# The first 768-token block's second product by seven block products, and its combined weights made four stages earlier

## The chip, the cores and the metric

The kernel runs on one core of a Trainium2 chip. The core has five instruction queues that run side by side and wait for each other through semaphores: TensorE (PE, matrix products into PSUM banks), VectorE (DVE), ScalarE (ACT), GpSimd (POOL) and SyncE (SP). Here SP issues all the transfers between the chip's memory (HBM) and the on-chip buffer (SBUF). Each engine takes its instructions strictly in the order in which they were written for it. The metric is the device time of one execution in microseconds (us); the time of a kernel is the median over its runs.

## The reference, cut to what matters

Pooled attention (keys and values are averaged over groups of 8) followed by a two-layer product with a gate between. Everything is float32.

```python
k_p = k.reshape(B, H, Sp, 8, D).mean(axis=3)          # B=8, H=8, Sp=72, D=64
v_p = v.reshape(B, H, Sp, 8, D).mean(axis=3)
attn = softmax(q @ k_p.T / sqrt(D))                    # 576 queries per head
x = (attn @ v_p) -> 4608 tokens x 512
h = x @ w_in                                           # 512 x 2048
g = h * clip(h + 3, 0, 6) / 6
out = g @ w_out                                        # 2048 x 512
```

## The kernel before, in words

The 4608 tokens are worked in blocks: `BLOCKS = [512, 256, 384, 384] + [384] * 8`. The first four blocks, numbered 0 to 3, are "plain"; the last eight are taken in pairs of 384 as four 768-token blocks. PE does its products on float32 data that have been rounded to a shorter form, so each operand is split into a rounded part (`hi`, written by ACT) and the remainder (`lo`, `q` minus `hi`, written by DVE), and each product is three: hi·hi, hi·lo, lo·hi. Attention for later tokens is fed in small steps between the products of earlier blocks.

**Plain blocks.** `run` goes over 16 steps, one for each 128 of the 2048 hidden columns. A step has the first product (`Step.h`, L841, 12 products into one of two PSUM banks), its gate (`relu` on ACT L849, `gate` on DVE L853), its split (`hi` on ACT L857, `lo` on DVE L861), and two steps later the second product (`Step.out`, L872, three products for each 128 tokens). Before a block's first step its tokens must be split too: `split_x`, ACT L624 and DVE L625, which writes `xhi` and `xlo`. `hooks[j][u]` holds work that is called after step `u` of block `j`.

**768-token blocks.** Their first product, `h`, is done by the seven-product form of a 2x2 block product (L1134): three of the seven right-hand operands are raw blocks of the weights, four are sums and differences of blocks ("combined weights"). In the last three of these blocks the second product, `out`, is done by seven products too (`out_seven`, L1261, 28 pieces of 3 x 6 products of 128x256 elements, 504 in all). In the first of them it is done plainly (`out_plain`, L1188, 16 pieces of 6 x 3 products of 128x512, 288 in all). All weights that the 768-token blocks need lie in HBM, in `wd` (for `h`), `w2d` (raw, for `out`) and `w2t` (combined, for `out`), and are read back through two rings of buffers (`chunk`, L992).

**Who makes the combined weights.** Those for `h` are made by `sums_of`, in 16 halves: eight in block 2 and eight in block 3, at every second step. A half is, in one go, two additions (L939), four dependent mixes (L944), the rounded copy on ACT (L945), the remainder (L946), and four stores of 128 KB (L948). Its buffer `wq` exists once, so the next half's first addition waits until the stores have read it. Those for `out` are made by `combine` (L1017, L1020, L1022, L1023, stores L1026) while the first 768-token block does its plain `out`: they read the pieces that are loaded for `out` anyway. `plain_of` stores the raw weights of blocks 2 and 3's hooks to HBM (L951); nothing that it reads changes, so these stores can be issued early.

**What sets the order.** Up to step 3 of block 1 the order on each engine is a written list. After it, the order comes from the scheduler of the language, which places each engine's instructions by its own estimate of when they are ready. `after_mark` adds the rule that an instruction stands behind the last marked one (the split of the latest step) on its engine. The SBUF that block 1's pool `early_x0` occupied is handed to the pool `early_x1` of blocks 2 and 3 when block 1's last step is reached; a tile that is put there waits for the last users of what lay there.

## Time and profile before

| | us |
|---|---|
| median of 3 runs (lowest to highest) | 893.26 (893.08 to 894.79) |
| the profiled execution | 893.88 |
| its span, first to last instruction | 892.1 |
| PE busy / DVE busy / ACT busy in the span | 869.2 / 665.9 / 553.6 |
| block 0 | 0 to 126 |
| block 1 | 126 to 184 |
| block 2 | 184 to 269 |
| block 3 | 269 to 346 |
| first 768-token block: `h`, then plain `out` | 346 to 423, 423 to 494 |
| second: `h`, `out` by seven | 494 to 566, 566 to 633 |
| third: `h`, `out` by seven | 633 to 704, 704 to 769 |
| fourth: `h`, `out` by seven | 769 to 828, 828 to 888 |

The stages' edges are the first products of the lines named above. The profile is of one execution; its rows give an engine, a line of the kernel, an operation, the tiles written and read, and busy time. A row of a timeline begins with its start and its length in us. A row of a table by stages gives a stretch of the span, its length, the busy time of PE, of its weight loads (PEld), of DVE, ACT and POOL, each with the count of instructions, then the granted share of the PE clock, the mean busy share of the 16 transfer engines, and GB/s.

### The profile page before, as it was taken

Reading aid. Unit: us, or ns where it says so; the run is one execution under the profiler, and the core shown is the slowest. Engines: PE = TensorE matmul, PEld = TensorE weight load, DVE = VectorE, ACT = ScalarE, POOL = GpSimd, SP = SyncE. Lnnn points to the kernel's source line nnn. Section 1 sums busy time; section 2 is a strip of 40 time slices with the busy share of each in tenths; the row PEclk is TensorE's granted clock in tenths of the full one; section 3 lists DMA queues with packets and bytes.
Section 4 is the critical chain, followed back from the end, with each engine's and each line's share of the span. In section 5 each row is a group of like instructions: output and inputs, shape, how many; then the busy total and the mean of one; then the engine's idle time right before and its main releaser. Section 6 shows DMA issues by size and latency. Waiting matters only on the chain.

```text
span 892.1 us, 15646 instructions
## 1 busy us (share of the span) xinstructions
PE 869.2 (97%) x5360; PEld 812.3 (91%) x5360; DVE 665.9 (75%) x1340; ACT 553.6 (62%) x1515; POOL 83.6 (9%) x168
## 2 busy tenths in 40 slices
PE   7899999999999999999999999999999999999998
PEld 6788888988989998998888999999999999999998
DVE  6999864567877785869788688897597877466664
ACT  5998766655656655778344688665577746355442
POOL 4100002110211100102000101100100200000000
PEclk9999999999999999999999999999999999999999
DMA  9970205995425234996587968877976777877873
GB/s 294 392 293 1 72 24 192 360 327 167 130 67 160 71 129 135 368 315 225 180 271 239 383 218 295 265 239 236 331 250 213 226 233 240 275 253 238 266 264 132
DMA packets 124654, 200.00 MB, mean 224 GB/s; under 512 B 13216, under 2 KB 81056, under 8 KB 124576
## 3 DMA queue, kind: packets, MB, share of 16 engines
q1 hardware_dynamic: 124432, 199.00, 67.8%
q8 instruction: 43, 0.70, 0.3%
q14 instruction: 35, 0.29, 0.1%
q10 hardware_dynamic: 144, 0.00, 0.0%
HBM read 158.08 MB, written 40.89 MB: 223 GB/s over the span
## 4 chain that ended last, share of the span: by engine, by line
PE 80%; DVE 8%; DMA 5%; ACT 4%; issue 2%; SPq 1%; POOL 0%; DVEq 0%; ACTq 0%; POOLq 0%
PE psx L1134 22%; PE psx L1261 19%; PE pso L872 12%; PE psh L841 12%; PE psx L1188 7%; PE psa L646 3%; PE psa L463 3%; ACT e L472 2%; PE psa L572 1%; DMA raw<-w_in_l 1%; DMA raw<-w_out_l 1%; DMA wd<-wq 1%; DVE vst L383 1%; DMA wsFalse<-wd 1%; DVE wq L939 1%
## 5 line engine op out<-in xcount | busy, mean ns | idle before, releaser
L1134 PE MATMUL psx<-x,wsFalse 128*128 128x384 f32 x768 | 151.8, 341 | 1.7 <-DVE g L1098 0.8
L841 PE MATMUL psh<-xhi,w 128*128 128x384 f32 (+2 forms) x520 | 145.9, 340 | 0.5 <-DVE g L853 0.4
L1134 PEld LDWEIGHTS psx<-x,wsFalse 128*128 128x128 f32 x768 | 133.6, 188 | 3.2 <-ACT c L1107 1.3
L1113 ACT CAST part<-g 128x768 fp32r<-128x768 f32 x100 | 83.3, 836 | 85.0 <-PE psx L1261 65.8
L1115 DVE TENSOR_TENSOR part<-g,part 128x768 fp32r<-128x768 f32 x100 | 95.2, 955 | 46.5 <-ACT part L1113 46.1
L872 PE MATMUL pso<-w,ghi 128*128 128x512 f32 x384 | 120.7, 398 | 0.4 <-ACT o L877 0.4
L1134 PE MATMUL psx<-x,wsTrue 128*128 128x384 f32 x576 | 115.8, 342 | 2.4 <-DMA wsTrue<-wd 2.3
L1261 PE MATMUL psx<-wsFalse,part 128*128 128x256 f32 x864 | 108.3, 282 | 1.5 <-DVE part L1115 1.1
L1261 PEld LDWEIGHTS psx<-wsFalse,part 128*128 128x128 f32 x864 | 105.2, 189 | 2.3 <-DVE part L1115 1.3
L1134 PEld LDWEIGHTS psx<-x,wsTrue 128*128 128x128 f32 x576 | 99.6, 188 | 3.1 <-DVE g L1092 3.1
L841 PEld LDWEIGHTS psh<-xhi,w 128*128 128x128 f32 x520 | 93.2, 188 | 8.2 <-DVE g L853 1.1
L472 ACT ACTIVATE e<-psa,mx 128x72 f32<-128x72 f32 x256 | 78.6, 324 | 23.7 <-DVE mx L467 22.4
L841 PE MATMUL psh<-xlo,w 128*128 128x384 f32 (+2 forms) x260 | 87.1, 336 | 0.0
L501 POOL TENSOR_TENSOR a<-e,sm 128x256 f32<-128x256 f32 x60 | 41.0, 683 | 478.3 <-DVE sm L490 377.9
L1261 PE MATMUL psx<-wsTrue,part 128*128 128x256 f32 x648 | 81.3, 283 | 0.0
L1261 PEld LDWEIGHTS psx<-wsTrue,part 128*128 128x128 f32 x648 | 79.3, 191 | 0.2 <-DVE part L1115 0.2
L872 PEld LDWEIGHTS pso<-w,ghi 128*128 128x128 f32 x384 | 69.1, 188 | 11.2 <-ACT o L877 0.7
L1090 ACT ACTIVATE r<-g,small 128x384 f32<-128x384 f32 x96 | 58.8, 621 | 28.4 <-DVE g L1098 28.0
L872 PE MATMUL pso<-w,glo 128*128 128x512 f32 x192 | 74.4, 399 | 0.0
L1098 DVE TENSOR_TENSOR g<-psx,c 128x384 f32<-128x384 f32 x96 | 52.3, 553 | 28.7 <-PE psx L1134 20.6
L1107 ACT COPY c<-psx 128x384 f32<-128x384 f32 x96 | 45.0, 485 | 28.5 <-PE psx L1134 28.1
L1092 DVE SCALAR_TENSOR_TENSOR g<-r,g 128x384 f32<-128x384 f32 x96 | 54.5, 576 | 9.7 <-ACT r L1090 9.2
(139 smaller groups left out, 1473.2 us busy)
## 6 DMA issues: line engine op xcount, KB each, us to landing
wsFalse<-wd SPq DMA_DIRECT2D x64, 512.0 KB, 4.6
wsTrue<-wd SPq DMA_DIRECT2D x48, 512.0 KB, 4.9
wsFalse<-w2d SPq DMA_DIRECT2D x31, 512.0 KB, 5.0
wsFalse<-w2t SPq DMA_DIRECT2D x27, 512.0 KB, 5.0
wsTrue<-w2d SPq DMA_DIRECT2D x21, 512.0 KB, 5.0
wsTrue<-w2t SPq DMA_DIRECT2D x21, 512.0 KB, 4.9
raw<-w_in_l SPq DMA_DIRECT2D x16, 512.0 KB, 8.6
raw<-w_out_l SPq DMA_DIRECT2D x16, 512.0 KB, 9.2
```

What stands on the lines that cost most here:

```text
L472: nc.scalar.activation(self.e[:, h], self.ps[:, h], AF.Exp, bias=self.mx[:, h : h + 1], accum_out=self.sm[:, h : h + 1])
L841: nc.tensor.matmul(self.ps, l[f][:, c, :], r[:, c, :], start=c == 0 and i == 0, stop=c == NCC - 1 and i == 2)
L872: nc.tensor.matmul(pos, l, r, start=f == 0 and i == 0, stop=f == NF - 1 and i == 2)
L1090: nc.scalar.activation(r, src, AF.Relu, bias=half_low, scale=GSCALE / (6.0 * WSCALE))
L1092: nc.vector.scalar_tensor_tensor(out=g_of[i][:, k], in0=r, scalar=GSCALE, in1=src, op0=ALU.min, op1=ALU.mult)
L1098: nc.vector.tensor_tensor(out=g_of[i][:, k], in0=ps, in1=kept, op=ALU.add)
L1107: nc.scalar.copy(c, ps)
L1113: nc.scalar.copy(t[:, 0], src)
L1115: nc.vector.tensor_tensor(out=t[:, 1], in0=src, in1=t[:, 0].bitcast(F32), op=ALU.subtract)
L1134: nc.tensor.matmul(ps, w[:, l, c * P : (c + 1) * P], t[:, r, c], start=o in (1, 2, 5) and c == 0 and k == 0, stop=c == 1 and k == 2, skip_ ...
L1188: nc.tensor.matmul(to, l, w[:, qs, r], start=f == 0 and k == 0, stop=end and k == 2)
L1261: nc.tensor.matmul(to, t[:, l, k, i * P : (i + 1) * P], w[:, k, r], start=begin and k == 0 and y == 0 and i % 2 == 0, stop=m == NM - 1 and ...
```

## The change

All four 768-token blocks do `out` by seven products; `out_plain` and `combine` are gone. The combined weights for `out` are now made from the resident weights in block 3 (`sums_of_out`, eight pieces of 4 x 128x256, in buffers of steps that block 3 has finished with). The combined weights for `h` move earlier: the first half of them (four whole pieces of 128x512 additions, through the space of `xlo` of block 0) into block 1, the second half (eight halves as before) into block 2. Each is cut in two parts: additions, mixes and the rounded copy after step `u`, remainder and stores after step `u+1`, ahead of that step's other hook work. The remainder is written by two instructions, and `sums_of` issues eight stores instead of four. Block 1's `xhi` and `xlo` lie together in the space of block 0's `xhi`.

```diff
-SEVEN = (1, 2, 3)
-MAKE = (range(8), (), (), ())
-TURN = (0, 2, 4, 6, 7, 9, 10, 12)
-TAIL = 5
...
+            elif j == 1:
+                t = early_x[-1].tile([P, 2, NCC, max(BLOCKS) // 2], dtype, name="x01", tag="xhi", bufs=1)
+                xs[j, "xhi"], xs[j, "xlo"] = t[:, 0], t[:, 1]
...
+    def sums(blocks, mixes, hi, q):
+
+        for r, (high, low) in enumerate(blocks):
+            nc.vector.tensor_tensor(out=q[:, 2 * r : 2 * r + 2], in0=high, in1=low, op=ALU.add)
             after_mark()
+        for to, a, b, how in mixes:
             nc.vector.tensor_tensor(out=q[:, to], in0=q[:, a], in1=q[:, b], op=how)
+            after_mark()
         nc.scalar.copy(hi.bitcast(F32R), q)
-        nc.vector.tensor_tensor(out=q.bitcast(F32R), in0=q, in1=hi, op=ALU.subtract)
-        for o, at in {7: 0, 3: 1, 5: 2, 6: 3}.items():
-            nc.sync.dma_start(dram_of(i, o)[:, :, half], t[:, :, at])
+    def low_of(hi, q):
+        for x in (slice(0, 2), slice(2, 4)):
+            nc.vector.tensor_tensor(out=q[:, x].bitcast(F32R), in0=q[:, x], in1=hi[:, x], op=ALU.subtract)
+            after_mark()
...
+    def sums_of(i, at, place):
+
+        hi, q = place()
...
+        sums(blocks, ((0, 0, 2, sub), (2, 2, 3, add), (3, 3, 0, sub), (1, 1, 3, sub)), hi, q)
+
+        def rest():
+            low_of(hi, q)
+            for o, x in {7: 0, 3: 1, 5: 2, 6: 3}.items():
+                for m, t in enumerate((hi, q)):
+                    nc.sync.dma_start(dram_of(i, o)[:, m, at], t[:, x])
+
+        return rest
+
+    def sums_of_out(i, place):
...
+        def rest():
+            low_of(hi, q)
+            for m, t in enumerate((hi, q)):
+                nc.sync.dma_start(w2t_dram[i // 2][:, :, i % 2, m], t)
...
-        (out_seven if n in SEVEN else out_plain)(n, j, bank, parts, split_g, split_f, pairs, second_att, rest, last_h)
+        out_of(n, j, bank, parts, split_g, pairs, second_att, rest, last_h)
...
+    def in_two(j, u, make):
+
+        rest = []
+        hooks[j].setdefault(u, []).append(lambda: rest.append(make()))
+        hooks[j].setdefault(u + 1, []).insert(0, lambda: rest.pop()())
+
+    for i, u in enumerate((4, 7, 10, 13)):
+        in_two(1, u, lambda i=i: sums_of(i, every, lambda: early_room(2 * P, "xlo")))
+    for n in range(8):
+        in_two(2, 2 * n, lambda n=n: sums_of(4 + n // 2, halves[n % 2], lambda: early_room(P, "wq")))
     plain = [lambda i=i, n=n: plain_of(i, n) for i in range(NPR) for n in range(4)]
-    for n, step in enumerate(make):
-        hooks[2 + n // NPR].setdefault(2 * (n % NPR), []).append(step)
     for n, step in enumerate(plain):
         hooks[2 + n // 16].setdefault(n % 16 // (1 + n // 16), []).append(step)
+    for i, (u, f) in enumerate(((0, 0), (2, 0), (3, 1), (5, 2), (6, 3), (8, 4), (10, 8), (12, 9))):
+        in_two(3, u, lambda i=i, f=f: sums_of_out(i, lambda: room(f)))
```

Because the scheduler sets the order, the diff does not show where the moved work lands. Two places are shown; the names after `wq` and `w` are buffer numbers, and the changed kernel's lines stand some lines lower or higher than the old ones (L941 to L948 became L933 to L966, L951 became L989, L625 became L622).

The first is the transfer queue on SP, around the last raw stores (`w2d`, `wd` from `w`), which in the old kernel are the last work ahead of block 2's first half. Before:

```order
L951 DMA wd_119<-w_1212 128x2x256
L241 DMA qt<-q_l 128x4x128
L288 DMA vst<-vr_l 32x2x256 x3
L951 DMA w2d_123<-w_1196 128x2x256 x2
L249 DMA kst<-k_l 128x576
L951 DMA w2d_123<-w_1263 128x2x256 x2
L241 DMA qt<-q_l 128x4x64
L249 DMA kst<-k_l 128x576
L878 DMA out<-o 128x512
L948 DMA wd_95<-wq 128x2x128
```

Now:

```order
L989 DMA wd_119<-w_1212 128x2x256
L989 DMA w2d_123<-w_1196 128x2x256
L237 DMA qt<-q_l 128x4x64
L989 DMA w2d_123<-w_1196 128x2x256
L989 DMA w2d_123<-w_1263 128x2x256 x2
L966 DMA wd_102<-wq 128x256
L966 DMA wd_101<-wq 128x256
L966 DMA wd_102<-wq 128x256
L966 DMA wd_101<-wq 128x256
L966 DMA wd_99<-wq 128x256 x2
L966 DMA wd_100<-wq 128x256 x2
```

Behind the last raw store stand now the eight stores of block 1's third combined piece, and behind them (not shown) the eight of its fourth. The stores of its first and second piece stand among the raw stores further up: 13 transfers from the first raw store come ahead of the first piece's eight, 23 more ahead of the second piece's, and 32 more ahead of the third's.

The second place is DVE at the end of block 1; `g` and `glo` are the gate and the split of a step (128x256 in block 1, 128x384 in block 2), `xlo` is block 2's split of its tokens. Before:

```order
L853 SCALAR_TENSOR_TENSOR g<-g,psh 128x256 [waits Activation_49]
L625 TENSOR_TENSOR xlo<-x,xhi 128x384 [waits PE_49,Activation_49]
L625 TENSOR_TENSOR xlo<-x,xhi 128x384 [waits Activation_49] x3
L861 TENSOR_TENSOR glo<-g,ghi 128x256 [waits Activation_49]
L467 TENSOR_REDUCE mx<-psa 128x4 [waits PE_49] x2
```

Now, the third piece (its additions read `w_653` and `w_696`) and, after some attention work, the fourth:

```order
L850 SCALAR_TENSOR_TENSOR g<-g,psh 128x256 [waits Activation_49]
L858 TENSOR_TENSOR glo<-g,ghi 128x256 [waits Activation_49]
L933 TENSOR_TENSOR wq<-w_653 128x512 [waits DMAHW4_49,DMAHW5_49,DMAHW3_49,DMAHW6_49,DMAHW2_49,DMAHW7_49,DMAHW1_49,DMAHW0_49]
L933 TENSOR_TENSOR wq<-w_696 128x512
L936 TENSOR_TENSOR wq<-wq 128x256 [waits DVE_49] x3
L463 TENSOR_REDUCE mx<-psa 128x4 [waits PE_49]
```

```order
L933 TENSOR_TENSOR wq<-w_743 128x512 [waits DMAHW4_49,DMAHW5_49,DMAHW3_49,DMAHW6_49,DMAHW2_49,DMAHW7_49,DMAHW1_49,DMAHW0_49]
L933 TENSOR_TENSOR wq<-w_821 128x512
L936 TENSOR_TENSOR wq<-wq 128x256 [waits DVE_49] x4
L942 TENSOR_TENSOR wq<-wq 128x512 [waits Activation_49]
L942 TENSOR_TENSOR wq<-wq 128x512
L622 TENSOR_TENSOR xlo<-x,xhi 128x384 [waits DMAHW3_49,DMAHW4_49,DMAHW2_49,DMAHW5_49,DMAHW1_49,DMAHW6_49,DMAHW0_49,DMAHW7_49,DVE_49,Activation_49]
L622 TENSOR_TENSOR xlo<-x,xhi 128x384 [waits Activation_49] x3
```

Both pieces now stand behind the last gate of block 1 and ahead of block 2's `xlo`. The eight `DMAHW` semaphores are those of transfers: followed to the transfers that raise them, the fourth piece's first addition waits for the third piece's eight stores, and block 2's first `xlo` for the fourth piece's eight stores, since it is put where the combined pieces lay.

More of the change, by code (lines that the diff above doesn't have):

```diff
@@ new lines, in room @@
+    def room(f):
+        if f:
+            t = const(f).tile([P, 2, 4, 2 * P], F32, name="wq", tag=f"w_{f}")
+            return t[:, 0], t[:, 1]
+        return (
+            early_x[-1].tile([P, 4, 2 * P], F32, name="wq", bufs=1),
+            const(0).tile([P, 4, 2 * P], F32, name="wq", tag="w_0_0"),
+        )
+    def sums_of(i, at, place):
+        hi, q = place()
+        blocks = [(w[:, 0, :, at], w[:, 1, :, at]) for w in pair_of(i)]
+        sub, add = ALU.subtract, ALU.add
+        sums(blocks, ((0, 0, 2, sub), (2, 2, 3, add), (3, 3, 0, sub), (1, 1, 3, sub)), hi, q)
[5 more added lines that the diff above has]
+        return rest
@@ new lines, in sums_of_out @@
+    def sums_of_out(i, place):
+        hi, q = place()
+        blocks = [w_of[2 * i + r, 1].bitcast(F32).rearrange("p m (q c) -> p m q c", q=2) for r in range(2)]
+        sub, add = ALU.subtract, ALU.add
+        sums([(w[:, 0], w[:, 1]) for w in blocks], ((3, 3, 1, sub), (1, 1, 0, sub), (0, 0, 3, add), (2, 2, 0, sub)), hi, q)
+        def rest():
+            low_of(hi, q)
+            for m, t in enumerate((hi, q)):
+                nc.sync.dma_start(w2t_dram[i // 2][:, :, i % 2, m], t)
+        return rest
@@ L1156, in super_block @@
         att_banks[:] = ["a0", "a1"]
-        (out_seven if n in SEVEN else out_plain)(n, j, bank, parts, split_g, split_f, pairs, second_att, rest, last_h)
+        out_of(n, j, bank, parts, split_g, pairs, second_att, rest, last_h)
         assert not rest
-    def out_plain(n, j, bank, parts, split_g, split_f, pairs, att, rest, last_h):
-        NT2 = 2 * HALF // P
-        paced = Paced(att, NT2 * (NF - TAIL))
-        split_f(0)
-        banks = ["o0", "h0", "o2", "o1", "h1", "o3"]
-        sums, outs = {}, []
-        for f in range(NF):
-            if f + 1 < NF:
-                split_f(f + 1)
-            w = next_w2(n, f)
-            for i in MAKE[n]:
-                if f == TURN[i]:
-                    combine(n, i)
-            for t in range(NT2):
-                if f < NF - TAIL:
-                    paced.slot()
-                elif rest:
-                    rest.pop(0)()
-                hi, lo = (parts[f][:, m].rearrange("p h t -> p (h t)")[:, t * P : (t + 1) * P] for m in range(2))
-                products = (hi, 0), (hi, 1), (lo, 0)
-                end = f == NF - 1
-                if f == 0:
-                    sums[t] = [(slice(0, 2), bank(banks, t, DM))]
-                    if n == len(supers) - 1 and t == NT2 - 1:
-                        sums[t] = [(slice(0, 1), sums[t][0][1][:, :256]), (slice(1, 2), bank(["a0"], 0, 256))]
-                for qs, pos in sums[t]:
-                    for k, (l, r) in enumerate(products):
-                        to = pos.rearrange("p (q c) -> p q c", c=DM // 2)
-                        nc.tensor.matmul(to, l, w[:, qs, r], start=f == 0 and k == 0, stop=end and k == 2)
-                        if f == 0 and k == 0:
-                            behind(traced[-1], last_h)
-                if not end:
-                    continue
-                if t % 3 == 0:
-                    o3 = late[1].tile([P, 4 * HALF], F32, name="o", tag="part", bufs=3)
-                o = o3[:, t % 3 * DM : (t % 3 + 1) * DM]
-                at = starts[j] + t * P
-                for x, (qs, pos) in enumerate(sums[t]):
-                    cols = slice(qs.start * 256, qs.stop * 256)
-                    (nc.vector.tensor_copy if (t + x) % 2 else nc.scalar.copy)(o[:, cols], pos)
-                    nc.sync.dma_start(out[at : at + P, cols], o[:, cols])
-            if f == NF - TAIL - 1:
-                paced.upto(len(paced.steps))
@@ L1204, in out_seven, with out_of @@
-    def out_seven(n, j, bank, parts, split_g, split_f, pairs, att, rest, last_h):
+    def out_of(n, j, bank, parts, split_g, pairs, att, rest, last_h):
         NT2, NM, W2 = HALF // P, NF // 4, DM // 2
```

64 lines of the change are left out of this document (16 added, 48 removed).

## The prediction

> **What bounds the kernel now.** I read the first table of the page first, then the shares of the chain of waits.
>
> ```profile
> span 892.1 us, 15646 instructions
> PE 869.2 (97%) x5360; PEld 812.3 (91%) x5360; DVE 665.9 (75%) x1340; ACT 553.6 (62%) x1515; POOL 83.6 (9%) x168
> PE 80%; DVE 8%; DMA 5%; ACT 4%; issue 2%; SPq 1%; POOL 0%; DVEq 0%; ACTq 0%; POOLq 0%
> ```
>
> PE is busy for all but 23 us, so the kernel is its stream of products; a change gains by fewer PE cycles, and loses wherever it makes PE wait. The busy time by stages shows where other engines or transfers come near. In order: block 1, block 2, block 3, the plain `out`, an `out` by seven, and the last one.
>
> ```profile
> 126.00:183.60 57.60, 57.60 (x376) 52.57 (x375) 33.42 (x93) 38.06 (x149) 11.99 (x24) 1.00 0.74 247
> 183.60:269.10 85.50, 83.19 (x446) 74.27 (x445) 63.94 (x172) 49.22 (x166) 11.04 (x20) 1.00 0.54 158
> 269.10:345.60 76.50, 76.50 (x411) 69.94 (x411) 57.71 (x138) 45.09 (x137) 7.11 (x14) 1.00 0.39 116
> 423.20:493.90 70.70, 70.70 (x328) 58.28 (x327) 57.94 (x98) 30.47 (x50) 1.97 (x4) 1.00 0.74 237
> 565.50:632.90 67.40, 66.12 (x539) 65.34 (x538) 52.86 (x79) 36.67 (x70) 2.05 (x5) 1.00 0.78 252
> 828.10:888.40 60.30, 60.30 (x506) 60.03 (x504) 37.01 (x45) 24.94 (x35) 0.00 (x0) 1.00 0.68 225
> ```
>
> PE is full in blocks 1 and 3, lacks 2.3 us in block 2, and DVE has room: 24 us in block 1, 19 in block 3. That speaks for moving DVE work there. What the means hide is the transfer queue around the edge from block 1 to block 2, which I looked at next.
>
> ```profile
> 150.00:190.00 40.00, 40.00 (x257) 36.77 (x256) 24.06 (x66) 25.82 (x100) 6.71 (x14) 1.00 1.04 354
> 190.00:200.00 10.00, 8.75 (x51) 7.34 (x50) 6.95 (x19) 5.99 (x26) 2.35 (x5) 1.00 0.96 307
> ```
>
> From 150 to 200 us the transfer engines are full (shares 1.04 and 0.96; 354 GB/s). The queue's own rows say with what:
>
> ```profile
> 148.15 1.66 SPq L951 DMA_DIRECT2D wd<-w  x3
> ...
> 156.97 3.13 SPq L951 DMA_DIRECT2D w2d<-w  x4
> ...
> 173.30 2.32 SPq L951 DMA_DIRECT2D wd<-w  x3
> 175.66 3.11 SPq L951 DMA_DIRECT2D w2d<-w  x4
> ...
> 197.36 1.29 SPq L951 DMA_DIRECT2D w2d<-w  x2
> 198.75 0.57 SPq L241 DMA_DIRECT2D qt<-q_l  x1
> ```
>
> These are the raw stores, 148.15 to 198.65, back to back. They hurt nobody in the old kernel, because nothing that PE needs soon stands behind them.
>
> **The change part by part.** *Plain products out, seven in.* The chain has long unbroken runs of both forms.
>
> ```profile
> 464.96 28.36 PE psx L1188 x123
> 828.34 59.47 PE psx L1261 x498
> ```
>
> Plain: 28.36/123 = 0.2306 us, times 288 = 66.4. Seven: 59.47/498 = 0.1194, times 504 = 60.2. The gain is 6.2; other stretches of either form move it between 4.9 and 7.0 (the lower end takes the second block's `out`, 67.4 less the 1.3 that PE idled, against 70.7: attention in it differs).
>
> *The combined pieces of block 1.* This term decides. The order rows on DVE put the third and the fourth piece behind block 1's last gate and ahead of block 2's `xlo`; the fourth's first addition waits for the third's eight stores, and `xlo` for the fourth's. On SP the third's stores stand behind every raw store. On PE, `xlo` is needed two products into block 2:
>
> ```profile
> 186.14 0.51 PE L841 MATMUL psh<-xhi,w 128*128 128x384 f32 x2
> 184.49 1.96 DVE L625 TENSOR_TENSOR xlo<-x,xhi 128x384 fp32r<-128x384 f32 x4
> ```
>
> Behind those products stand, on PE, all of block 2's first step and its attention; behind `xlo` on DVE, block 2's gates. So PE stops until four pieces, through one buffer, have left through a queue that is full. Durations: `L1017`, `L1020`, `L1022` are the same shapes as a whole piece's; a remainder of 128x512 is the 717 of `L946`; a store's landing is the page's median from issue.
>
> ```profile
> L1017 DVE TENSOR_TENSOR tq<-wsFalse 128x512 f32<-128x512 f32 x8 | 5.2, 686 | 1.2 <-issue 1.2
> L1020 DVE TENSOR_TENSOR tq<-tq 128x256 f32<-128x256 f32 x20 | 8.4, 421 | 0.2
> L1022 ACT CAST th<-tq 128x1024 fp32r<-128x1024 f32 x5 | 5.2, 1049 | 6.2 <-DVE tq L1020 6.2
> L946 DVE TENSOR_TENSOR wq<-wq 128x512 fp32r<-128x512 f32 x16 | 11.5, 717 | 5.5 <-ACT wq L945 5.2
> w2d<-w SPq DMA_DIRECT2D x32, 256.0 KB, 4.7
> wd<-wq SPq DMA_DIRECT2D x64, 128.0 KB, 2.0
> ```
>
> On the old kernel's clock:
> - Raw stores start at 148.15. Thirteen transfers take until 158.5 (two of the four in the row at 156.97); then the first piece's eight stores, 8 x 128 KB = 1.05 MB at 354 GB/s = 3.0: 161.5.
> - Twenty-three more, 158.5 to 175.6 in the old kernel, 17.1: 178.6. The second piece's stores, 3.0: 181.6.
> - Thirty-two more, 175.66 to about 199.3, 23.7: 205.3. The last raw store lands 4.7 later, 210.0; the third piece's stores 3.0 behind it, 213.0.
> - The fourth piece: two additions 1.4, four mixes 1.7, rounded copy 1.05, two remainders 1.4, with hand-overs 218.5. Its stores, about 1 to issue and 2.0 to land: 221.5. The first quarter of `xlo`, 1.96/4: 222.0.
>
> Against 186.14 that is 35.9 later. Some work goes into the gap: two steps' second products of block 1 (1.4, already counted as done in the old kernel by 186.14, but written later in the new one) and attention ready by then (four products took 0.65 in the old kernel; I estimate 2.4 in all from that row's pitch), together 3.8. And the idle 1.25 of 190 to 200 (8.75 busy of 10.00) is swallowed. The term: 35.9 - 3.8 - 1.3 = 30.8. Bounds: if the raw stores and the two first pieces share the engines without lengthening the queue (the 6.0 of their stores falls out) it is 24.8, if landings also overlap 22.8; if the attention transfers that the queue now holds are not made up for, and attention cannot fill the gap, 34.6.
>
> *PE's restart.* PE will have idled for some 30 us. The only such start in the trace is the beginning:
>
> ```profile
> 2.37 4.96 PE L326 MATMUL idle<-ident 128*128 128x128 f32 x26 [2.37 <-POOL ident masks.py:199]
> 10.41 0.83 PE L326 MATMUL idle<-ident 128*128 128x128 f32 x6
> ```
>
> 0.191 each against 0.138: 26 x 0.053 = 1.4 lost. I take 1.4, bounds 0 and 1.9 (were the first products here all of the longer, 384-element form). The Trainium skill ("TensorE: Matmul & The Clock Gate", section "Part 1: The HAM clock gate") says that PE after an idle window of about 3.4 us runs at half clock for about 3.4 us; by that 1.7 would be lost and the sum would be 0.3 higher. The trace agrees in direction, though the profile grants 1.00 throughout.
>
> *Blocks 2 and 3.* Old halves:
>
> ```profile
> L939 DVE TENSOR_TENSOR wq<-w 128x256 f32<-128x256 f32 x32 | 13.5, 462 | 10.0 <-DMA wd<-wq 9.8
> L944 DVE TENSOR_TENSOR wq<-wq 128x128 f32<-128x128 f32 x64 | 18.8, 293 | 1.2
> ```
>
> A half is 2 x 0.462 + 4 x 0.293 + 0.717 = 2.81, eight are 22.5. A piece for `out` is 2 x 0.686 + 4 x 0.421 + 2 x 0.717 = 4.49, eight are 35.9. Block 3's DVE goes from 57.7 to 71.1 of 76.5 (93%). At that load a gate comes late now and then, and block 2, at 64 of 85.5 with the same halves, already lacks 2.3. The cover is that a piece's two parts stand behind a step's split. I take +3 for both blocks; bounds 0 (what block 3 lacks now) and 10 (the 71.1 plus the 5.5 that `L946` waits and the 10.0 that `L939` waits exceeds 76.5 by this much).
>
> *The start of the first 768-token block.* There PE waits for a chunk of combined weights:
>
> ```profile
> 353.22 5.34 DMA wsTrue<-wd
> ```
>
> That is 2.3 idle, since the load waits for the last half's stores in block 3. These are now made in block 2, so the wait goes: -2, bounds -2.5 and 0. `combine` leaves the DVE of the first `out`, where PE was full anyway: 0; if PE starved on the seven form's loads there as it does in the second block's, +1.3, inside the range.
>
> Sum against the profiled execution's 893.9: - 6.2 + 30.8 + 1.4 + 3 - 2 = 920.9. The median of the runs lies 0.6 below that execution, which is within the rounding of these terms: 921.
>
> **The rivals.**
> - *The queue keeps up.* As above, but the stores of the first pieces slip in between the raw ones at no cost, so that `xlo` comes at 216 or earlier. For: piece stores are on other buffers, and 307 GB/s at 190 to 200 leaves something. Against: a share of 1.04. 921 - 6 to 8 = 914.
> - *DVE becomes the bound in block 3* on top of the gap: +10 in place of +3, so 928; with halves late in block 2 as well, 931. For: 93%. Against: steps leave DVE's order loose by two.
> - *No gap; the change works as written.* The other side: the third piece's stores would land while block 1 is still in its products, by 184. From there it decides: whatever lands by then costs PE nothing. Then 893.9 - 6.2 + 1 (block 3's DVE) - 2 = 887. For: PE, DVE and SP would all follow `hooks` (steps 4, 7, 10 and 13 of block 1's sixteen). Against: the order rows put pieces three and four last on their engines, and the raw stores take 50 us whatever else happens; started at 148 they cannot be gone by 184.
> - *DVE alone holds block 2* (pieces late, but no store waited for): the fourth piece would end by about 195 and cost 9; that is 899. The waits on the stores stand in the rows, so it has no chance of its own; the range leaves it out.
>
> **How the numbers follow.** The gap as worked out 0.72; the queue keeps up 0.12; DVE the bound as well 0.08; no gap 0.08. The predicted time is the first's. Low end: the gap at 22.8, no restart loss, blocks 2 and 3 at 0, the rest at its best (-7.0 and -2.5) give 907, so 908. High end: 34.6, 1.9, +3 and 0 for the first block's start with a gain of 4.9 give 928.5, and DVE's case 931: I stop at 930. This kernel's runs can tell about 0.2% (1.8 us) from no change. Faster by more than that is the case without a gap but for a share in which the small terms eat the gain: 0.07, with 0.01 within 0.2%; slower 0.92.
>
> **What would show it.** The gap: in the changed kernel's rows PE's first `psh<-xhi,w` of 384 elements comes near 217 to 222, idle before it some 30 us, put down to `xlo` on DVE, and that to transfers `wd<-wq`; the last raw store's row ends near 205 and the third piece's first store follows it. Block 1's first part stays as it was. The restart: the first products behind the gap take longer than the same products later in block 2. Block 3: DVE near 71 busy, PE lacking up to 3. The first `out`: 504 products of about 0.119. The start of the first 768-token block: no idle of 2.3. Wrong would be: a first `psh` of block 2 by 190, or an idle ahead of it that ends with something other than `xlo`; or raw stores that start well before 148 or end well before 199.

## The result

| | us |
|---|---|
| before, median | 894.02 (893.08 to 895.79) |
| changed, median | 929.6 (928.68 to 930.67) |
| ratio | 1.040, 95% interval 1.0385 to 1.0416 |
| forecast | 921, range 908 to 930 |

The change makes the kernel 4% slower, at the upper end of the range. The first tables of the changed kernel's profile, its span of 926.8 against 892.1:

```profile
span 926.8 us, 16228 instructions
PE 871.9 (94%) x5576; PEld 823.9 (89%) x5576; DVE 686.7 (74%) x1365; ACT 564.8 (61%) x1528; POOL 84.5 (9%) x168
PE 72%; DVE 10%; DMA 7%; ACT 4%; SPq 3%; issue 2%; DVEq 0%; POOL 0%; ACTq 0%
```

PE is busy 2.7 us longer, but idle 55 us in place of 23. The stages, taken from the times at which PE starts the first product of each, say where:

| stage | before | changed | difference |
|---|---|---|---|
| block 1 up to block 2's first product | 60.1 | 93.5 | +33.4 |
| block 2 | 83.0 | 83.6 | +0.6 |
| block 3 | 76.5 | 81.2 | +4.7 |
| first 768-token block, `h` | 77.7 | 79.3 | +1.7 |
| its `out` | 70.8 | 65.5 | -5.3 |

Together 35.1; what lies ahead of block 1 is 0.3 shorter, and the later stages differ by 0.2 or less. So nearly all of it is one place, the edge from block 1 to block 2. Two rows need care, because a stage is cut at the next one's first product. Block 2 holds a wait of 5.6 us that belongs to the edge, and makes up for it with attention that PE did while it waited. And in the changed kernel 18 of block 3's second products stand behind the first product of `h`, in the old one 9: these nine are 2.1 us, so the 1.7 by which `h` grew are block 3's. PE idles in that `h` as long as before (3.7 us against 3.6). In the changed kernel's queue of transfers (start, length, line, operation, count) the rows that answer to those of before are these; L989 are the raw stores, L966 the combined ones:

```profile
148.24 1.49 SPq L989 DMA_DIRECT2D wd<-w  x3
...
158.41 5.29 SPq L966 DMA_DIRECT2D wd<-wq  x8
...
180.43 4.68 SPq L966 DMA_DIRECT2D wd<-wq  x8
...
206.25 1.92 SPq L989 DMA_DIRECT2D w2d<-w  x3
208.26 14.54 SPq L966 DMA_DIRECT2D wd<-wq  x16
```

The first piece's eight stores go at 158.4, the second's at 180.4, and the third's and fourth's behind the last raw store, from 208.3 to 222.8. DVE, in its own timeline, waits for them twice:

```profile
214.52 1.29 DVE L933 TENSOR_TENSOR wq<-w 128x512 f32<-128x512 f32 x2 [16.04 <-DMA wd<-wq]
215.85 1.81 DVE L936 TENSOR_TENSOR wq<-wq 128x256 f32<-128x256 f32 x4
218.81 1.30 DVE L942 TENSOR_TENSOR wq<-wq 128x512 fp32r<-128x512 f32 x2 [1.16 <-ACT wq L938]
225.22 1.97 DVE L622 TENSOR_TENSOR xlo<-x,xhi 128x384 fp32r<-128x384 f32 x4 [5.11 <-DMA wd<-wq]
```

The fourth piece's additions idle 16.0 us for the third's stores, and block 2's `xlo` 5.1 us for the fourth's. PE's waits between 186 and 227 us (waiting operation, what it waited for, total, times, longest) are the other end of it:

```profile
PE psh L838 <- ACT xhi L621: 20.8, 1, 20.8
PE psh L838 <- DVE xlo L622: 5.6, 1, 5.6
PE psa L568 <- ACT e L468: 2.5, 1, 2.5
```

ACT is named first because its `xhi` stands on ACT behind the fourth piece's rounded copy, which ACT could not start before 217.7; the reason for both is the buffer. ACT's timeline has the two:

```profile
217.73 1.04 ACT L938 CAST wq<-wq 128x1024 fp32r<-128x1024 f32 x1 [19.58 <-DVE wq L936]
218.68 1.75 ACT L621 CAST xhi<-x 128x384 fp32r<-128x384 f32 x4
```

Busy time by stretches (length, PE, PEld, DVE, ACT, POOL, granted clock, transfer share, GB/s) of the changed kernel, for the gap, the 77 us behind it, block 3's two halves and the first `out`:

```profile
187.30:225.83 38.53, 6.78 (x26) 4.61 (x25) 12.16 (x31) 8.22 (x29) 2.00 (x5) 0.60 0.78 253
225.80:302.80 77.00, 76.06 (x404) 69.49 (x405) 55.40 (x155) 41.46 (x134) 7.98 (x15) 0.98 0.33 94
302.86:345.00 42.14, 41.19 (x227) 37.25 (x226) 35.18 (x88) 25.52 (x91) 6.84 (x12) 1.00 0.49 158
345.00:384.01 39.01, 36.35 (x175) 32.27 (x175) 36.75 (x68) 22.09 (x41) 0.99 (x2) 0.96 0.51 169
463.35:525.87 62.52, 62.32 (x523) 62.12 (x523) 49.43 (x72) 35.62 (x72) 3.11 (x4) 1.00 0.73 233
```

In the gap PE has 6.8 us of work in 38.5, all of it attention but for block 2's first two products. Block 2 behind it is nearly full (76.1 of 77.0). In block 3's second half DVE has 36.8 us of work in 39.0, and PE loses 2.7. The first `out` by seven is full on PE.

### The profile page after: what moved, and what is told of

Read it like the earlier page. It is cut to its first block, busy times and chain, and to the rows that moved or that the text cites. A ratio compares the mean times of both kernels' runs of the same rounds, so it can differ in the third digit from the quotient of the medians.

```text
span 926.8 us, 16228 instructions
## 1 busy us (share of the span) xinstructions
PE 871.9 (94%) x5576; PEld 823.9 (89%) x5576; DVE 686.7 (74%) x1365; ACT 564.8 (61%) x1528; POOL 84.5 (9%) x168
## 4 chain that ended last, share of the span: by engine, by line
PE 72%; DVE 10%; DMA 7%; ACT 4%; SPq 3%; issue 2%; DVEq 0%; POOL 0%; ACTq 0%
PE psx L1228 24%; PE psx L1145 22%; PE psh L838 10%; PE pso L869 9%; PE psa L643 3%; PE psa L459 2%; DMA wd<-wq 2%; SPq L966 2%; SPq L989 1%; ACT e L468 1%; DMA raw<-w_in_l 1%; DMA raw<-w_out_l 1%; DVE vst L379 1%; PE psa L568 1%; DVE wq L936 1%
## 5 line engine op out<-in xcount | busy, mean ns | idle before, releaser
L1127 ACT CAST part<-g 128x768 fp32r<-128x768 f32 x112 | 93.6, 837 | 88.3 <-PE psx L1228 86.4
L838 PE MATMUL psh<-xhi,w 128*128 128x384 f32 (+2 forms) x392 | 121.8, 365 | 24.4 <-ACT xhi L621 20.8
L1129 DVE TENSOR_TENSOR part<-g,part 128x768 fp32r<-128x768 f32 x112 | 106.7, 956 | 51.0 <-ACT part L1127 50.7
L1228 PE MATMUL psx<-wsFalse,part 128*128 128x256 f32 x1152 | 143.7, 282 | 0.2 <-DVE part L1129 0.2
L1228 PEld LDWEIGHTS psx<-wsFalse,part 128*128 128x128 f32 x1152 | 139.8, 189 | 0.4 <-DVE part L1129 0.4
L1228 PE MATMUL psx<-wsTrue,part 128*128 128x256 f32 x864 | 110.5, 283 | 1.7 <-DVE part L1129 1.1
L1228 PEld LDWEIGHTS psx<-wsTrue,part 128*128 128x128 f32 x864 | 106.4, 191 | 2.7 <-ACT kept L1203 1.4
L838 PEld LDWEIGHTS psh<-xhi,w 128*128 128x128 f32 x392 | 73.8, 192 | 32.7 <-ACT xhi L621 21.2
L869 PEld LDWEIGHTS pso<-w,ghi 128*128 128x128 f32 x384 | 69.8, 189 | 11.1
L838 PE MATMUL psh<-xlo,w 128*128 128x384 f32 (+2 forms) x196 | 70.1, 358 | 5.6 <-DVE xlo L622 5.6
L869 PE MATMUL pso<-w,glo 128*128 128x512 f32 x192 | 71.8, 395 | 0.0
L846 ACT ACTIVATE g<-psh,small 128x384 f32<-128x384 f32 (+2 forms) x65 | 37.8, 582 | 44.9 <-DVE glo L858 22.0
```

What stands on the lines that cost most here:

```text
L838: nc.tensor.matmul(self.ps, l[f][:, c, :], r[:, c, :], start=c == 0 and i == 0, stop=c == NCC - 1 and i == 2)
L846: nc.scalar.activation(self.g, self.ps, AF.Relu, bias=half, scale=1.0 / (6.0 * WSCALE))
L869: nc.tensor.matmul(pos, l, r, start=f == 0 and i == 0, stop=f == NF - 1 and i == 2)
L1127: nc.scalar.copy(t[:, 0], src)
L1129: nc.vector.tensor_tensor(out=t[:, 1], in0=src, in1=t[:, 0].bitcast(F32), op=ALU.subtract)
L1228: nc.tensor.matmul(to, t[:, l, k, i * P : (i + 1) * P], w[:, k, r], start=begin and k == 0 and y == 0 and i % 2 == 0, stop=m == NM - 1 and ...
```

## The experiments

Four questions were open. Is the gap the queue, the buffer, or the work of the pieces? What is the seven-product form worth alone? What made block 3 and the first `h` longer? And can the gain be had without the gap? In the diffs a line that begins with + or - is added to or taken from the changed kernel unless another is named. The stages of all kernels:

| kernel | median | block 1 to edge | block 2 | block 3 | first `h` | first `out` |
|---|---|---|---|---|---|---|
| before | 894.0 | 60.1 | 83.0 | 76.5 | 77.7 | 70.8 |
| changed | 929.6 | 93.5 | 83.6 | 81.2 | 79.3 | 65.5 |
| raw stores behind | 905.8 | 71.2 | 82.2 | 80.9 | 81.6 | 65.5 |
| ... behind block 1's alone | 911.2 | 71.4 | 87.6 | 83.7 | 78.6 | 66.3 |
| buffer free | 908.3 | 66.7 | 89.6 | 80.4 | 79.7 | 65.5 |
| both | 898.0 | 66.7 | 77.7 | 81.7 | 81.1 | 65.5 |
| block 1's stores alone | 906.1 | 61.6 | 93.9 | 79.1 | 82.5 | 65.6 |
| plain first `out` | 937.4 | 92.9 | 85.4 | 81.7 | 81.3 | 71.7 |
| halves as before, GpSimd helps | 922.2 | 60.1 | 82.8 | 93.4 | 94.4 | 66.2 |
| halves as before, DVE alone | 920.1 | 60.1 | 83.2 | 80.2 | 108.1 | 65.1 |
| raw stores behind, four stores a piece | 906.0 | 70.6 | 80.4 | 82.9 | 82.1 | 65.8 |
| ... three pieces, ten halves | 891.8 | 61.0 | 79.2 | 80.8 | 79.5 | 65.5 |
| ... pieces for `out` earlier | 897.6 | 61.0 | 79.1 | 83.6 | 80.6 | 65.5 |
| ... three, ten, 75% attention | 887.7 | 61.0 | 78.9 | 80.5 | 75.7 | 65.9 |

The medians are of several runs, the stages of one profiled execution each.

### The queue cured: raw stores behind the combined ones

```diff
         nc.sync.dma_start(dram_of(i, o)[:, m, at], t[:, x])
+        made[:] = [traced[-1].name]
...
     def store(to, src):
         nc.sync.dma_start(to, src)
+        behind(traced[-1], made[0])
```

> The changed kernel, with every raw store put on SP's queue behind the combined stores that are written ahead of it in the program; buffers and DVE work as they are. Theory Q (the gap is made by the combined pieces' one buffer being emptied through a queue full of raw stores): the gap goes; block 1 and the edge last about 60 to 62 us up to block 2's first product (93.5 in the changed kernel, 60.1 in the old), and the kernel takes 888 to 897: 893.9 - 5.3 by the seven-product out, + 0.6 in block 2, and + 4.7 in block 3 and + 1.7 in the first 768-token h if these two don't come from the gap. Rival D (the pieces' own additions, mixes and copies, some 6 us each, hold DVE at the edge): at least 9 us of the gap stay, 900 or more. Rival S (what blocks 3 and the first h lost is the gap's aftermath): these two stages go back to 76.5 and 77.7 and the kernel takes about 889; if they stay long, S falls.

Measured: 905.84 us, 1.0125 of the old kernel (1.0094 to 1.0156). Two thirds of the gap (22.3 of 33.4 us) go, but 11.1 stay, so theory Q as worded fell, and D was right that at least 9 would stay; how much of them is DVE's own work is measured further down. The rows of this run's queue show each piece's stores going out as soon as they are made, and `xlo` on DVE still waiting for the fourth's:

```profile
179.85 4.59 SPq L966 DMA_DIRECT2D wd<-wq  x8
...
193.10 3.75 SPq L966 DMA_DIRECT2D wd<-wq  x8
```

```profile
186.34 1.29 DVE L933 TENSOR_TENSOR wq<-w 128x512 f32<-128x512 f32 x2 [1.28 <-DMA wd<-wq]
...
198.51 1.96 DVE L622 TENSOR_TENSOR xlo<-x,xhi 128x384 fp32r<-128x384 f32 x4 [1.94 <-DMA wd<-wq]
```

The fourth piece starts at 186.3, when block 1's products are all but done. Rival S fell: without the large gap block 3 still takes 80.9 and the first `h` 81.6.

### The same for block 1's pieces alone

```diff
-        made[:] = [traced[-1].name]
+        if at == every:
+            made[:] = [traced[-1].name]
```

(against the kernel before this one: the raw stores stand behind block 1's pieces, but ahead of block 2's halves).

> As the run before, but the raw stores are only put behind block 1's four pieces; behind these they may go out at once. Theory Q: no gap at the edge (60 to 62 us), but now block 2's combined halves, through one buffer, stand behind raw stores, some 30 of them ahead of the third half's: PE loses 5 to 20 us inside block 2 (83.6 in the changed kernel), so 895 to 912. Rival D: the gap at the edge stays above 9 us whatever the queue does, and block 2 is as it was.

Measured: 911.21 us (ratio 1.0152 to 1.0216). The edge is as in the run before, 71.4, where Q had 60 to 62, and block 2 is 5.5 us longer than there (87.6 against 82.2). So stores behind the raw ones cost PE in block 2 as well, but not the combined ones alone: PE's longest wait there, 4.0 us, ends with ACT's copy of an output block `o`, and ACT had waited 8.8 us for the store of the output block before it (`out<-o`), which stood behind raw stores. DVE waits 11.2 us for the halves' stores at the same time. The next run shows the same two waits, with its rows.

### The buffer cured: stores read the raw weights

```diff
+        src = pair_of(i)[m][:, 0, 0, at] if at == every else None
-        nc.sync.dma_start(dram_of(i, o)[:, m, at], t[:, x])
+        nc.sync.dma_start(dram_of(i, o)[:, m, at], t[:, x] if src is None else src)
```

> The changed kernel, with block 1's 32 combined stores reading the raw weights instead of the combined pieces (the same number and bytes of transfers; the combined weights of four pieces are not stored, so the output isn't the reference's). The queue is as full, but no store holds the buffer. Theory Q: the gap goes (60 to 62 us to block 2's first product) though the raw stores still run from 148 to above 200; in block 2 the halves still stand behind them, so up to 10 us there; 889 to 905. Were the queue alone at fault (transfers that attention needs come late, without the buffer), the gap would stay at 20 us or more. Rival D: 9 us or more of it stay.

Block 1's combined weights are then missing from HBM; the transfers are as many and as large. Measured: 908.32 us, edge 66.7, block 2 89.6. With the queue as full as ever and no store holding the buffer, 26.8 of the 33.4 us at the edge go. The 6.6 that stay lie below D's 9, and above the 60 to 62 us of Q. Part of the gap only moved: in block 2 PE loses 9.3 us in one wait (the waits of PE from 195 to 225 us; behind them what ACT and DVE waited for):

```profile
PE pso L869 <- ACT o L874: 9.3, 1, 9.3
PE psh L838 <- DVE g L850: 0.4, 1, 0.4
```

```profile
220.57 0.60 ACT L874 ACTIVATE o<-pso 128x512 f32<-128x512 f32 x1 [14.07 <-DMA out<-o]
222.86 0.76 DVE L933 TENSOR_TENSOR wq<-w 128x256 f32<-128x256 f32 x2 [15.78 <-DMA wd<-wq]
```

PE waits for ACT to empty a PSUM bank into `o`, and ACT for the store of the block before, which stood in the queue behind raw stores. DVE, with block 2's gates behind it, waits 15.8 us for the first half's stores and starts 2.3 us after ACT. So two other buffers are emptied behind the burst; by these rows either alone would have held PE for about as long.

### Both, and neither but the stores

The first and the third edit in one kernel, the queue and the buffer cured:

> Both cures at once: raw stores behind the combined ones on SP, and block 1's combined stores reading the raw weights, so that no store holds the buffer (four pieces of combined weights are not stored: not the reference's output). Behind the two runs of one cure each, 11.1 us (queue cured) and 6.6 us (buffer cured) were left at the edge of block 1 against the old kernel's 60.1. Theory R (what is left is the pieces' own DVE and ACT work between block 1's gates, 6.6, and the buffer's round trip with an empty queue, 4.5): the edge lasts 66 to 67 us. Theory T (the 6.6 left with a free buffer were attention's transfers, late behind raw stores): it lasts 60 to 62.5.

And block 1 with only the stores:

```diff
+    def stores_of(i):
+        for o in (7, 3, 5, 6):
+            for m in range(2):
+                nc.sync.dma_start(dram_of(i, o)[:, m], pair_of(i)[m][:, 0, 0])
...
     for i, u in enumerate((4, 7, 10, 13)):
-        in_two(1, u, lambda i=i: sums_of(i, every, lambda: early_room(2 * P, "xlo")))
+        hooks[1].setdefault(u + 1, []).append(lambda i=i: stores_of(i))
```

> The changed kernel without block 1's combined pieces: no additions, mixes, copies or remainders there, but the same 32 stores, at the same steps, reading raw weights (four pieces of combined weights are missing from the output's making). Theory R: the edge goes back to 60 to 61.5 us. Theory T: 66 us or more, as when only the buffer was free. In block 2 the halves' one buffer still stands behind raw stores: 83 to 90 us; blocks 3 and the first h tell whether they are long without any gap ahead of them (80 to 81 and 79 to 82, as in all four kernels so far) or not.

Measured: with both 898.0 us and an edge of 66.7, as theory R said; with the stores alone 906.1 and 61.6, 0.1 above R's range. Theory T fell. So the edge's 33.4 us split, cured in this order: 22.3 go with the full queue (93.5 to 71.2), 4.5 with the one buffer when the queue is empty (71.2 to 66.7), 5.1 with the pieces' own work on DVE and ACT (66.7 with the buffer free, 61.6 with the stores alone, both under a full queue), and 1.5 stay.

The small parts of this are not all lost time. With both cures PE does 13 more attention products and 6 more second products ahead of the edge than in the old kernel, and block 2, with as many fewer and 1.5 us less idle, is 5.3 us shorter; with the stores alone PE does not idle at all up to the edge, and the 1.5 are 13 attention products done early. Block 1's stage and block 2 together take 143.1 us in the old kernel; the changed kernel takes 34.0 more, with the queue cured 10.2, with both cured 1.3. By this count the queue is 23.8, the buffer with an empty queue 8.9, and the pieces' own work, net, 1.3.

The stores-alone kernel has its wait in block 2, which takes 93.9 where 83 to 90 was expected: PE waits 14.0 us for ACT's `o`. ACT's row and DVE's are those of the run with the buffer free again, and longer.

```profile
219.98 0.60 ACT L874 ACTIVATE o<-pso 128x512 f32<-128x512 f32 x1 [19.04 <-DMA out<-o]
221.76 0.76 DVE L933 TENSOR_TENSOR wq<-w 128x256 f32<-128x256 f32 x2 [20.23 <-DMA wd<-wq]
```

### The seven-product form alone

The changed kernel with `out_plain` of the old one for the first 768-token block:

```diff
-        out_of(n, j, bank, parts, split_g, pairs, second_att, rest, last_h)
+        if n:
+            out_of(n, j, bank, parts, split_g, pairs, second_att, rest, last_h)
+        else:
+            out_plain(n, j, bank, parts, split_g, split_f, pairs, second_att, rest, last_h)
```

> The changed kernel with the first 768-token block's out done plainly again (288 products of 128x512, raw weights read back), the combined weights made as in the changed kernel. This alone is what the seven-product form is worth. By the forecast's term of 6.2, or by the stage lengths of the two traces (5.3), the kernel takes 935 to 936; the gap is as it was (93.5 us from block 1's first product to block 2's). If the seven-product form gained nothing here, because loads or splits bind it, 930.

Measured: 937.37 us, 7.8 more than the changed kernel by the medians; the stage itself is 6.2 longer (71.7 against 65.5). Block 2 and the first `h` are 1.8 and 1.9 longer too, the `h` at a granted clock of 0.97 in place of 1.00; neither has the form in it. The gap is as it was (92.9). The gain of the form is real, 5.3 by the old kernel's stage and 6.2 by this one's.

### The combined weights for `h` left where they were

Eight halves in block 2 and eight in block 3, in one go, as in the old kernel; the pieces for `out` in block 3, of which GpSimd makes five:

```diff
+    for n, step in enumerate(make):
+        hooks[2 + n // NPR].setdefault((0, 2, 4, 6, 8, 10, 12, 14, 2, 4, 5, 7, 9, 10, 12, 13)[n], []).append(step)
...
+    for i, (u, f, e) in enumerate(((0, 0, 1), (3, 1, 0), (5, 2, 0), (7, 3, 0), (8, 4, 0), (11, 8, 0), (12, 9, 1), (13, 10, 1))):
+        in_two(3, u, lambda i=i, f=f, e=e: sums_of_out(i, lambda: room(f), nc.vector if e else nc.gpsimd))
```

> A version meant to keep the gain and leave block 1 alone: all four blocks do out by seven, the h halves are made as in the old kernel (eight in block 2, eight in block 3, one go each), and of the eight combined pieces for out in block 3 GpSimd makes five and DVE three. Block 1's edge and block 2 are as in the old kernel (60.1 and 83.0). DVE in block 3: 57.7 + 3 x 4.5 = 71 of 76.5, as in the changed kernel, so block 3 costs 0 to 4.7. The first out 65.5 in place of 70.8. Sum 886 to 893, 889 the likeliest. If GpSimd's long instructions hold DVE up where both work, block 3 costs over 5 and it is no better than the old kernel.

and with DVE for all eight:

> The same, but DVE makes all eight pieces for out in block 3, together with the eight h halves there: 57.7 + 35.9 = 93.6 us of DVE work in a block of 76.5. Theory: DVE becomes the bound, block 3 takes 90 to 94, and the kernel 901 to 906. If less (pieces slide into the first 768-token h, whose DVE has room), 892 to 900.

Measured: 922.2 and 920.1 us, both far above what was expected (886 to 893, and 901 to 906). Block 1 and block 2 are as in the old kernel (60.1; 82.8 and 83.2): the gap needs the pieces in block 1. But block 3 and the first `h` pay: 93.4 and 94.4 with GpSimd, 80.2 and 108.1 with DVE alone. In the second kernel the theory had the place wrong: the surplus slides out of block 3, and PE stops once for 18.2 us in `h`, put down to an evacuation on ACT (`c`), while DVE finishes the last halves. The rows of ACT and DVE carry this one step further:

```profile
375.83 0.76 DVE L971 TENSOR_TENSOR wq<-w 128x256 f32<-128x256 f32 x2 [4.16 <-DMA wd<-wq]
377.97 0.62 ACT L977 CAST wq<-wq 128x512 fp32r<-128x512 f32 x1 [7.03 <-DVE wq L976]
378.50 0.47 ACT L1119 COPY c<-psx 128x384 f32<-128x384 f32 x1
```

`c` stands on ACT behind the rounded copies of the last three halves (363.2, 370.3, 378.0), and each half's first addition waits for the stores of the half before to leave the one buffer. It is the pattern of block 1's edge again, without a full queue. In the first kernel the rival came true that the expectation had named. Groups of DVE instructions from 290 to 345 us, in the GpSimd kernel:

```profile
L976 DVE TENSOR_TENSOR wq<-wq 128x128 f32<-128x128 f32 x17 | 10.4, 615 | 0.5
L858 DVE TENSOR_TENSOR glo<-g,ghi 128x384 fp32r<-128x384 f32 x9 | 8.7, 966 | 0.6 <-ACT ghi L854 0.6
L850 DVE SCALAR_TENSOR_TENSOR g<-g,psh 128x384 f32<-128x384 f32 x8 | 4.4, 549 | 0.7 <-ACT g L846 0.6
```

and the same in the old kernel:

```profile
L861 DVE TENSOR_TENSOR glo<-g,ghi 128x384 fp32r<-128x384 f32 x12 | 6.7, 554 | 1.8 <-ACT ghi L857 1.8
L853 DVE SCALAR_TENSOR_TENSOR g<-g,psh 128x384 f32<-128x384 f32 x12 | 6.6, 553 | 4.4 <-ACT g L849 4.4
L944 DVE TENSOR_TENSOR wq<-wq 128x128 f32<-128x128 f32 x20 | 5.8, 288 | 0.3
```

With GpSimd's additions beside them, DVE's operations with two SBUF operands take 615 ns in place of 288 and 966 in place of 554; the gate, which reads PSUM, stays at 549 (553 in the old kernel's rows). In the same stretch of the kernel with DVE alone the three take 285, 553 and 549. While GpSimd works on its pieces (287 to 350 us), DVE's operations take 20 us longer in all than the medians of the same operations in that kernel; the five pieces would have been some 22 us of DVE work (5 x 4.49, an estimate from the old kernel's rows). So what GpSimd took over cost DVE nearly as much again.

### Towards a version without the gap

Raw stores behind the combined ones as above, and one store for both parts of a piece's block:

```diff
-            for m, t in enumerate((hi, q)):
-                nc.sync.dma_start(dram_of(i, o)[:, m, at], t[:, x])
+            nc.sync.dma_start(dram_of(i, o)[:, :, at], t4[:, :, x])
```

> Raw stores behind the combined ones (as in the first cure, 905.8, whose stages to block 3 were 71.2 and 82.2), and four stores of both parts per piece in place of eight. The buffer's round trip with an empty queue gets shorter by some 1.5 to 2 us a piece (eight stores issue in 3.8 to 4.6, four should in about 2). Theory R (what was left with an empty queue is the round trip through one buffer, four times): the edge goes from 71.2 to 63 to 67, and the kernel takes 897 to 902. If the edge stays at 70 or more, the number of stores is nothing.

Measured: 905.96 us, edge 70.6 against 71.2, where R had 63 to 67. The count of stores is nothing. The fourth piece still starts when block 1 ends. Then three whole pieces in block 1, ten halves in block 2:

```diff
-    for i, u in enumerate((4, 7, 10, 13)):
+    for i, u in enumerate((4, 7, 10)):
...
-    for n in range(8):
-        in_two(2, 2 * n, lambda n=n: sums_of(4 + n // 2, halves[n % 2], lambda: early_room(P, "wq")))
+    for n, u in enumerate((0, 1, 3, 4, 6, 7, 9, 10, 12, 13)):
+        in_two(2, u, lambda n=n: sums_of(3 + n // 2, halves[n % 2], lambda: early_room(P, "wq")))
```

> As the run before, with three whole pieces in block 1 and ten halves in block 2 in place of four and eight. Theory R: no piece is left at the edge, 60.5 to 63 us; block 2, with 5.6 us more DVE work and ten round trips, 81 to 85; the kernel 892 to 898. The rest (block 3 at 80 to 82 and the first h at 79 to 82) stays, as nothing in them was changed.

Measured: 891.81 us against 893.14 of the old kernel in the same comparison, ratio 0.9992 (0.998 to 1.0004): no difference that can be told. The edge is 61.0, so the fourth piece alone was 9.6 of the last 10.5 us, and up to it PE does not idle; block 2, where 81 to 85 was expected, takes 79.2 and even gains 3.8 on the old kernel. Block 3 still loses 4.3 and the first `h` 1.8. PE's waits in block 3 are one of 2.8 us for an attention operand that GpSimd makes and two, 2.7 in all, for gates. On top of this, the pieces for `out` nearer to block 3's start:

```diff
-    for i, (u, f) in enumerate(((0, 0), (2, 0), (3, 1), (5, 2), (6, 3), (8, 4), (10, 8), (12, 9))):
+    for i, (u, f) in enumerate(((0, 0), (2, 0), (3, 1), (4, 2), (6, 3), (7, 4), (8, 5), (10, 8))):
```

> As the run before, with block 3's pieces for out nearer to its start (the last at step 10, not 12), away from the sums of tokens that DVE makes for the first 768-token block from step 11 on. Theory B (block 3's loss is DVE full in its last 25 us): the 2.5 us wait ahead of block 3's last step goes and block 3 takes 77 to 79.5; the kernel 1.5 to 4 us less than the run before, 889 to 895, so the first of these kernels that may beat the old one (893.5). If block 3 stays at 81, the loss has another cause.

Measured: 897.62 us (the profiled execution, 894.32, is the fastest of five), block 3 at 83.6: worse, and theory B as it was put fell. PE idles 6.6 us there against 5.6 before; 1.7 of the 2.8 us more are a lower granted clock, of which the last section has the rows. DVE's timeline is without a hole of 0.5 us from 328.7 to 345.5 there, the gates of 330.4, 337.1 and 343.6 standing between pieces and sums of tokens: the DVE work of block 3 (71.8 us by stretches in the kernel with three pieces) can be moved about inside it, but not away. Last, that kernel with 75% of the first block's attention beside `h` in place of 85%:

```diff
-CUTS = (.85, 0.85, 0.85, 0)
+CUTS = (.75, 0.85, 0.85, 0)
```

> The version with three pieces in block 1 and ten halves in block 2 (891.8), with 75% in place of 85% of the first 768-token block's attention steps beside its h, the rest beside its out. The first h is 79.5 us there against 77.7 in the old kernel (which also waits 2.5 for a load), and its last 25 us hold 21.5 us of DVE work and 3.2 us of PE waiting for DVE and ACT; its out is full on PE with DVE at 50 of 66. Theory: the attention steps moved away leave DVE free at the end of h, and as both stages count PE's work the same, the two together (145.8 us) lose 2 to 3 us: 888.5 to 890.5, faster than the old kernel by 0.3 to 0.5%. Rival: DVE's sums of gates for the seven-product out, not attention, hold the end of h; the two together stay at 145 to 146.5 and the kernel at 891 to 893.

Measured: 887.74 us against 893.76, ratio 0.9942 (0.9924 to 0.996): 0.6% faster than the old kernel, and by the ratios faster than the kernel with three pieces. The first `h` goes from 79.5 to 75.7, and `h` and `out` together lose 3.3 us, somewhat more than the 2 to 3 expected. What was left of the waits at the end of `h` is one of 0.7 us; the two stages by stretches, `h` and then `out`:

```profile
345.57:421.26 75.69, 74.26 (x441) 72.56 (x440) 62.48 (x146) 57.40 (x194) 12.29 (x24) 1.00 0.89 299
421.26:488.07 66.81, 66.61 (x560) 66.41 (x559) 53.05 (x83) 37.41 (x78) 3.43 (x6) 1.00 0.76 243
```

PE lacks 1.4 us in the first (3.6 in the old kernel's `h`) and 0.2 in the second.

## Why the prediction was right, and where it was off

- **The gap** (30.8, with the restart 32.2; measured 34.0: 33.4 at the edge and 0.6 in block 2). The chain went link by link as it was forecast: first piece's stores at 158.4 (158.5), second's at 180.4 (178.6), third's behind the last raw store at 208.3 (205.3), fourth piece at 214.5 (213.0), `xlo` at 225.2 (221.5). Two links were put too short. The queue ahead of the third piece ended 2.9 us later than forecast. And the fourth's eight stores were given 1 us to issue: `193.10 3.75 ... x8` of the run with an empty queue shows 3.75, and from the remainder's end at 220.1 to `xlo` at 225.2 it is 5.1, where 3.0 was put. One was put too long: from the third's first store to the fourth piece it is 6.2, where 7.7 was put. Of the 3.7 us by which `xlo` was later, 1.8 reached the sum: PE did 5.8 us of attention in the gap, at a granted clock of 0.60, where 2.4 had been estimated.
- **One sign of being wrong came true as it was worded.** The longest idle, 20.8 us, ends with `xhi` on ACT and not with `xlo`. The forecast took `xhi` to be on time and did not look at ACT's order, where it stands behind the fourth piece's rounded copy. It added nothing, since `xlo` came later still, held by the same buffer.
- **What the forecast had not seen in the gap.** It named the one buffer and the full queue together and gave neither a price of its own. The runs show 22.3 us at the edge from the queue, 4.5 from the one buffer with an empty queue, 6.6 from the rest; over block 1's stage and block 2 together 23.8, 8.9 and 1.3. At the edge the full queue hurts only through this buffer: with it free the edge is 66.7 under a full and under an empty queue alike. In block 2 it hurts through two more, the halves' and the output block's. DVE's own work, which the prediction had as a rival of 9 us without a chance, is 5.1 at the edge and 1.3 by the longer count.
- **The restart** (1.4). By stretches, the clock granted to PE behind the gap is 0.52 for 3.2 us and then 1.00:

```profile
225.80:229.00 3.20, 3.17 (x10) 3.17 (x11) 1.38 (x3) 0.00 (x0) 0.00 (x0) 0.52 0.00 0
229.00:231.00 2.00, 2.00 (x14) 1.97 (x12) 0.00 (x0) 0.02 (x1) 0.00 (x0) 1.00 0.00 0
```

  That is 1.5 us lost, as estimated. The Trainium skill ("TensorE: Matmul & The Clock Gate", section "Part 1: The HAM clock gate") has half clock for about 3.4 us, and here the trace agrees.
- **Seven products for the first `out`** (6.2, bounds 4.9 to 7.0): 5.3 against the old kernel, 6.2 against the changed kernel with the plain form. Inside its bounds.
- **Blocks 2 and 3** (+3, bounds 0 to 10): block 2's +0.6 is counted with the gap; block 3 is +4.7, and 6.8 with its nine products that fall into the stage of `h`. The DVE load was right (71 forecast; 71.9 in the two halves of block 3), the cost was put too low: PE idles 3.6 us, most of it for gates, and a lower granted clock takes 1.7 more. That DVE, with 36.8 us of work in the second half's 39.0, leaves two parts a step apart no room to hide is argued from these rows, not shown: the run that moved the pieces about did not take the loss away.
- **The start of the first `h`** (-2): the step that failed. The wait for the combined weights is gone, as forecast, but PE idles as long as before: waits for DVE's gates (1.7) and ACT's copies (2.1), most of it at the end of the stage, took its place. The 1.7 by which the stage grew are block 3's products. The run with 75% of the attention shows what the waits are: with less attention there they fall to 1.4, and the stage takes 75.7.
- **The rivals.** The time measured is that of the case with DVE as a second bound (928 with +10 in block 3), though block 3, its products in `h` counted, gave 6.8 and not 10. No gap, and a queue that keeps up, are excluded by the rows above.
- **The number.** The sum forecast 27.0 us more, the stages show 35.1: 1.8 of the difference is the gap, 5.4 are block 3 and the first `h` (+1 forecast for the two terms, +6.4 measured), 0.9 the seven products. All three erred to the same side. That the median stayed 0.4 us inside the range, and one of its four runs (930.67) did not, is luck. The mechanism of the main term is not: the runs above show it.

## What to carry to other kernels

A single buffer that is emptied by stores ties the engine that fills it to everything that stands ahead of those stores in the queue. A tile laid over that buffer ties the next stage to it too, and work that stands behind the filling on the same engine waits with it. Read the order of the queue, not only its load, before work is moved ahead of a burst that nobody waited for until then, and look for every buffer that is emptied behind the burst: here there were three. When a chain of pieces through one buffer ends at a stage's edge, taking the last piece away is worth far more (9.6 us here) than making its stores fewer (0.6). A stage's length alone misleads where work slides over its edge; count the products in it too. An engine at 75% in the mean can be full where it counts (DVE with 36.8 us of work in 39.0). And in this kernel, work handed to GpSimd cost DVE beside it nearly as much as it took over.

## What the hardware showed that was not expected

- With GpSimd's additions beside them DVE's take about twice as long, in the mean of 55 us: 288 to 615 ns and 554 to 966 ns for operations with both operands in SBUF, 553 to 549 for one that reads PSUM. The Trainium skill ("GPSIMD Engine Reference", section "1. Specifications") names this contention for DVE instructions with two SBUF inputs, and the trace agrees on which are hit; the size is the runs'.
- Waits of PE far below the gap's length cost clock too, but not always. Behind a wait of 2.4 us near the end of block 3 the changed kernel's next 6 us were granted 0.72; behind one of 2.3 us at the start of the old kernel's first `h` the clock stayed at 1.00:

```profile
378.00:384.00 6.00, 5.82 (x21) 5.33 (x22) 5.12 (x11) 2.66 (x5) 0.00 (x0) 0.72 0.13 45
```

```profile
358.50:362.00 3.50, 3.30 (x19) 3.33 (x20) 0.72 (x1) 1.59 (x3) 0.00 (x0) 1.00 1.09 365
```

  The kernel with the pieces for `out` earlier and the one with three pieces have the same wait of 2.8 us near block 3's start, for the same operand. Behind it the first was granted 0.72 and the second 1.00:

```profile
276.50:282.50 6.00, 5.83 (x23) 5.43 (x24) 5.38 (x18) 4.73 (x21) 2.06 (x5) 0.72 1.00 319
```

```profile
276.50:282.50 6.00, 5.84 (x33) 5.26 (x34) 5.72 (x18) 4.74 (x21) 2.06 (x5) 1.00 0.97 317
```

  So a wait of 2.4 to 2.8 us can cost 1.7 more (6.0 x 0.28), and its length alone does not decide. What does is open.
